# Token transform on even and odd tokens apart: 145 of 289 outputs computed, the rest by sum and difference

## The chip, the cores and the metric

The kernel runs on one core of one Trainium2 chip. The metric is the device time in microseconds (us); lower is better. A profile of one execution gives, beside it, the span from the first to the last instruction and what each engine did. The engines are PE (matrix multiply, with its weight loads shown as PEld), DVE (vector), ACT (scalar), POOL (GpSimd) and SP (which here only issues DMAs).

## What is computed

Two blocks follow each other. The first is attention within chunks of 64 tokens: q, k and v have shape (8 batches, 8 heads, 576 tokens, 64). The second takes the result as x with shape (8, 576, 512), mixes it by the real part of a two-dimensional Fourier transform, over tokens and over features, and puts a normalized two-layer MLP on top:

```python
scores = q_chunk @ k_chunk.T / sqrt(64)          # 64 x 64 for each chunk and head
x      = softmax(scores) @ v_chunk               # heads side by side: (8, 576, 512)
u      = x + real(fft(fft(x, axis=1), axis=2))
un     = (u - mean(u)) / sqrt(var(u) + 1e-6)     # over the 512 features
out    = u + relu(un @ w_ch1) @ w_ch2            # w_ch1 512 x 2048, w_ch2 2048 x 512
```

All of it is fp32 on the chip. The two weight matrices arrive as doubles and are rounded to fp32 on the chip.

## The kernel before, in words

**Tiles.** A tile is 128 tokens of one batch in 128 partitions, with 512 features. Of the 576 tokens of a batch, chunks 0 to 3 make two LO tiles, chunks 8 to 5 two HI tiles (tokens run the other way, and features mirrored), and chunk 4 is half of a RE (rest) tile that two batches share. That is 36 tiles: 16 LO, 16 HI, 4 RE. `CH` is 64, `NM` 2, `NQ` 289, `NL` 256, `HQ` 128, `DV` 65.

**Attention** of a tile (`attention_early` for batch 0, `attention` for the others) has four parts: `att_T` transposes q and k, `att_S` multiplies them (L384), `softmax` and `exponential` work on DVE and ACT, `att_P` transposes the probabilities on PE and copies them from PSUM with ACT (L416), and `att_V` multiplies by v (L432) and scales the result into `xall` with DVE. L384 and L432 use 64 x 64 pieces of the PE array: for each pair of heads four matmuls, two in rows by two in columns. From batch 2 on, `att_V` of a tile is followed directly by `att_S` of the next one.

**Fold.** `shift` puts token rows in order so that LO token t stands beside HI token 576 - t. `fold` then adds and subtracts LO and HI and their mirrored features, which makes `pm`: four blocks of 128 features (T = 0 to 3) for i = 0, 1, and `pm_rest` for the rest tile. One more column of `pm` holds the middle feature. It runs on POOL, on DVE for batch 1 and for the last fold of batch 0.

**Token transform.** `fourier(b)` multiplies each block by a table of cosines (T = 0, 1) or sines (T = 2, 3) for tokens 0 to 288 (L652). The rest tile contributes with 64 rows, the middle column with one-column matmuls whose results lie in four partition groups of one PSUM bank. ACT then copies the four results into `zf` (tokens 1 to 256) and `zr` (tokens 257 to 288 with their mirror) in L678 to L688, and `mixed` (L700) does the feature transform from those. The four results use both buffers of the PSUM pool `ps_t` and the double bank of `ps_a`. Batch 0 has its own version, `fourier_early`, whose copies are divided between ACT and DVE, with matmuls on zeros (`keep_warm`, L1167) put between the parts of the start.

**Tables.** `load_tables` brings the tables in by DMA on SP's queue, `turn_tables` (L252 to L254, ACT) turns their tokens round into `tk`.

**MLP and the order of the work.** Each group of four tiles goes through `mlp`: group 0 with plain products in both layers, group 1 in the first layer, all others with a seven-product scheme on half matrices (`up_halves`, L1040, and `down_halves`, L1089), whose operands are combined on DVE, ACT and POOL and whose weight pieces come from DRAM through `fetch`. The order is written out by hand: after each step of the MLP the loop at L1213 advances the work of a later batch (attention, three empty steps, `fourier`) by as many steps as are due between two times in `ready_at`. `fourier` gives control back after the products of T = 0 and 1, after the copies, and after each `mixed`. Weight rounding (`round_weight`, L308 to L323 on DVE, L300 to L306 on ACT) also runs from this loop until all pieces are done, at about 154 us.[...]

**Stores.** `store` writes a finished tile: one DMA for LO, two for HI, and for each half of a RE tile one of 63 rows and one of a single row (L882, L883). All are on SP's queue, but for half of the last group's RE stores, which are on ACT's. The last group, the four RE tiles, ends the kernel.

Of the kernel before, what the change touches and what calls it, by code (L numbers as in the profile page):

```python
# [16 lines left out]
def kernel(  # L17
# [67 lines left out]
    tk = const.tile([128, NM + 1, 2, NQ], FP32, name="tk")  # L85
# [84 lines left out]
    more_v = one_p.tile([128, 4 * NL + 64], FP32, tag="zf", name="more_v")  # L170
# [53 lines left out]
    def load_tables():  # L224

        t = start[:, 0:(NM + 1) * 2 * NQ].rearrange("p (i r f) -> p i r f", i=NM + 1, r=2)
        for c in range(2 * NM):  # L230
            (i, r0), (j, p0) = divmod(c * CH, 128), divmod((NC - 1 - c) * CH, 128)
            nc.sync.dma_start(out=t[r0:r0 + CH, i], in_=seq_tab[p0:p0 + CH, j])
        for r0 in (0, CH):
            nc.sync.dma_start(out=t[r0:r0 + 1, NM], in_=seq_tab[0:1, 0])
            nc.sync.dma_start(out=t[r0 + 1:r0 + CH, NM], in_=seq_tab[1:CH, NM])
        for i in range(2):
            nc.sync.dma_start(out=first_rest[32 + 32 * i:33 + 32 * i, 0:DM], in_=dim_tab[0:1, 1 + 2 * i, :])
# [9 lines left out]

    def turn_tables():
        t = start[:, 0:(NM + 1) * 2 * NQ]
        a, b = tk.rearrange("p i r f -> p (i r) f"), t.rearrange("p (i f) -> p i f", f=NQ)  # L250
        for c in range(2 * NM):
            nc.scalar.copy(a[:, :, c * CH:(c + 1) * CH], b[:, :, (c + 1) * CH:c * CH:-1])  # L252
        nc.scalar.copy(a[:, :, NL:NL + 1], b[:, :, 0:1])
        nc.scalar.copy(a[:, :, NL + 1:NQ], b[:, :, NL + 1:NQ])  # L254
# [157 lines left out]
    def att_P(n):  # L412
        ex = es.pop(n)
        pt = turn(lambda j: ex[:, j].rearrange("p e k -> p (e k)"))
        t = one_p.tile([128, NJ, 128], FP32, tag="pT", name="pT")
        nc.scalar.copy(t, pt)  # L416
        pT[n] = t

    def att_V(n):
# [5 lines left out]
        else:  # L425
            xp = ps_a.tile([128, 2, 512], FP32, tag="att", name="xp")
            xp = [xp[:, e] for e in range(2)], xp
        for j in range(NJ):
            for e in range(2):
                for c in range(2):  # L430
                    r0, t0 = e * CH, c * CH
                    nc.tensor.matmul(  # L432
                        out=xp[0][e][t0:t0 + CH, j * DV:(j + 1) * DV],
                        lhsT=a[r0:r0 + CH, j, t0:t0 + CH],
                        rhs=b[r0:r0 + CH, c, j, :],
                        start=True,
                        stop=True,
                    )
# [25 lines left out]
    def shift_early(i):  # L464
# [3 lines left out]
        if i == 0:  # L468
            nc.gpsimd.tensor_copy(kept, lows[1][0:1])
            nc.gpsimd.tensor_copy(lows[1][0:1], lows[1][CH:CH + 1])  # L470
            nc.gpsimd.tensor_copy(lows[1][CH:CH + 1], rest)
        else:
            nc.scalar.copy(rest, lows[0][0:1])
            nc.scalar.copy(lows[0][0:1], lows[0][CH:CH + 1])
            nc.scalar.copy(lows[0][CH:CH + 1], kept)

    def shift(b):
# [6 lines left out]
        for i in range(NM):  # L484
            eng.dma_start(out=t[2 * i:2 * i + 2, 0:DM], in_=lows[i][0:CH + 1:CH, 0:DM])
        eng.dma_start(out=t[2 * NM:2 * NM + 1, 0:DM], in_=rest)
        for i in range(NM):
            eng.dma_start(out=lows[i][0:CH + 1:CH, 0:DM], in_=t[2 * i + 1:2 * i + 3, 0:DM])
        eng.dma_start(out=rest, in_=t[0:1, 0:DM])

    def fold(b, i):
# [5 lines left out]
        else:  # L497
            two = one_p.tile([128, 2 * (HM + 1)], FP32, tag="two", name="two")
        if i < NM:
            pm = two_p.tile([128, DM + 1], FP32, tag="pm", name="pm")  # L500
# [5 lines left out]
        else:  # L506
            pm = two_p.tile([128, 2 * HQ + 1], FP32, tag="pm_rest", name="pm_rest")
# [10 lines left out]
        if i < NM:  # L518
# [3 lines left out]
            to = pm[:, 3 * HQ:DM + 1:HQ]  # L522
        else:
            for T, op in enumerate((ALU.add, ALU.subtract, ALU.subtract, ALU.add)):
                to = pm[T % 2 * CH:T % 2 * CH + CH, T // 2 * HQ:T // 2 * HQ + HQ]
                eng.tensor_tensor(out=to, in0=near[:, T // 2], in1=far[:, T // 2], op=op)
            to = pm[CH:, HQ:2 * HQ + 1:HQ]
        eng.tensor_copy(to, two[p, HM + 1 + HQ:HQ - 1:-HM - 1])
        pms[b, i] = pm

    def attention_early():
# [33 lines left out]
        turn_tables()  # L565
# [78 lines left out]
    def fourier(b):  # L644
        h = b % 2
        zf = one_p.tile([128, 4 * NL + 64], FP32, tag="zf", name="zf")
        zf = zf[:, 0:4 * NL].rearrange("p (t f) -> p t f", t=4)
        pm = [pms.pop((b, i)) for i in range(NM + 1)]

        def product(T, i, out_, lhsT, start, stop, cols=slice(0, NQ)):  # L650
            p = slice(0, 128) if i < NM else slice(T % 2 * CH, T % 2 * CH + CH)
            nc.tensor.matmul(  # L652
                out=out_, lhsT=lhsT[p], rhs=tk[p, i, T // 2 if T != 5 else 0, cols],
                start=start, stop=stop, skip_group_check=True,
            )


        z = [ps_t.tile([128, 512], FP32, tag="pt", name="z") for _ in range(2)]
        more = ps_a.tile([128, 2, 512], FP32, tag="att", name="more_z")
        z += [more[:, k] for k in range(2)]  # L660
        for T in range(4):
            for i in range(NM):
                product(T, i, z[T][:, 0:NQ], pm[i][:, T * HQ:(T + 1) * HQ], i == 0, False)
            if T == 1:
                yield
        for T in range(4):
            product(T, NM, z[T][:, 0:NQ], pm[NM][:, T // 2 * HQ:(T // 2 + 1) * HQ], False, True)

        mids = []
        for g, c0 in enumerate(range(0, NQ, NS)):  # L670
            c1 = min(c0 + NS, NQ)
            mids.append((c0, c1, z[2][32 * g:32 * g + 1, NQ:NQ + c1 - c0]))
        for i in range(NM + 1):
            for c0, c1, out_ in mids:
                one = pm[i][:, DM:DM + 1] if i < NM else pm[i][:, 2 * HQ:2 * HQ + 1]
                product(5, i, out_, one, i == 0, i == NM, slice(c0, c1))
        for T in range(4):
            nc.scalar.copy(zf[:, T, :], z[T][:, 0:NL])  # L678
            nc.scalar.copy(zr[:, T, h, 0:NQ - NL], z[T][:, NL:NQ])
            upper, mirrored = zr[:, T, h, NQ - NL:CH], z[T][:, NQ - 2:NL:-1]  # L680
            nc.scalar.activation(out=upper, in_=mirrored, func=ACTF.Copy, scale=1.0 if T < 2 else -1.0)
            for c0, c1, from_ in mids if T == 2 else ():
                n = max(0, min(c1, NL) - c0)
                if n > 0:
                    nc.scalar.copy(zf[0:1, T, c0:c0 + n], from_[:, 0:n])
                if c1 > NL:
                    nc.scalar.copy(zr[0:1, T, h, 0:NQ - NL], from_[:, n:])
                    nc.scalar.copy(zr[0:1, T, h, NQ - NL:CH], from_[:, NQ - 2 - c0:NL - c0:-1])  # L688
# [38 lines left out]
    def fourier_early():  # L727
# [3 lines left out]
        zf = one_p.tile([128, 4 * NL + 64], FP32, tag="zf", name="zf")  # L731
        zf = zf[:, 0:4 * NL].rearrange("p (t f) -> p t f", t=4)
        pm = [pms.pop((0, i)) for i in range(NM + 1)]
        z = [ps_t.tile([128, 512], FP32, tag="pt", name="z") for _ in range(2)]
        more = ps_a.tile([128, 2, 512], FP32, tag="att", name="more_z")
        z += [more[:, k] for k in range(2)]
        mid = ps_f.tile([128, 512], FP32, tag="ff", name="mid")
        mids = [(c0, min(c0 + NS, NQ)) for c0 in range(0, NQ, NS)]
        order = (1, 0, NM)
        for i in order:  # L740
            at_ = {"start": i == order[0], "stop": i == order[-1], "skip_group_check": True}
# [554 lines left out]
```

## Time and profile before

| what | value |
|---|---|
| device time, median of 3 runs | 1091.47 us (1090.56 to 1092.83) |
| span of the profiled execution (the page gives no other time of its own for it) | 1089.0 us |
| mean granted PE clock, share of full speed | 0.998 |
| PE busy | 1070.4 us, 98% |
| DVE busy | 577.2 us, 53% |
| ACT busy | 299.2 us, 27% |
| POOL busy | 280.3 us, 26% |
| DMA | 192.73 MB, mean 177 GB/s |
| chain that ended last: L1089 and L1040 together | 20% + 17% + 15% + 13% |
| same chain: L652, the token products | 2% + 1% |

Times in the profile's rows are in us from the start of the span. A row of the timeline has start, duration, engine, line, operation, out<-in by the program's names, shapes, and how many instructions were merged into it; a note in brackets is idle time of that engine just before, and what ended it. [...]the distance between starts is what one costs in a stream. "PEclk" is the granted clock.

### The profile page before, as it was taken

To read this page: it belongs to the slowest core of one execution; us is meant where nothing else is said; L and a number is where in the kernel's file an instruction comes from. 1 tells how busy PE (TensorE), PEld (TensorE's weight loads), DVE (VectorE), ACT (ScalarE), POOL (GpSimd) and SP (SyncE) were. 2 spreads that over 40 slices of the span, in tenths; PEclk is the share of its full clock that TensorE was granted. 3 is DMA by queue.
4 is the path that set the end of the run, shared out by engine and by line. 5 is a ranking of instruction groups with operands and counts; after the bars stand their busy time and mean duration, and the time that the engine had idled before them with its cause. 6 is when DMAs were issued, how large, how long until landed. Compare 5 with 4: busy or idle time off the path is not lost.

```text
span 1089.0 us, 18837 instructions
## 1 busy us (share of the span) xinstructions
PE 1070.4 (98%) x7018; PEld 848.7 (78%) x7018; DVE 577.2 (53%) x1258; ACT 299.2 (27%) x730; POOL 280.3 (26%) x403
## 2 busy tenths in 40 slices
PE   8999999999999999999999999999999999999998
PEld 6644454446888888888888888888888888888887
DVE  4899987314566355663556455735663534323411
ACT  4788453222113310322022212321133103101300
POOL 4301002444405140153114220514051401210140
PEclk9999999999999999999999999999999999999999
DMA  7777556679575637692668357854653455446232
GB/s 167 224 222 175 158 162 227 171 239 308 178 203 167 198 136 206 189 255 95 191 184 253 124 165 223 206 170 152 197 185 90 147 190 163 120 154 211 78 116 78
DMA packets 147970, 192.73 MB, mean 177 GB/s; under 512 B 66126, under 2 KB 104014, under 8 KB 140712
## 3 DMA queue, kind: packets, MB, share of 16 engines
q1 hardware_dynamic: 145620, 190.20, 58.4%
q8 instruction: 56, 0.92, 0.4%
q0 software_dynamic: 512, 0.68, 0.3%
q10 hardware_dynamic: 1748, 0.66, 0.2%
q14 instruction: 34, 0.28, 0.1%
HBM read 167.22 MB, written 24.12 MB: 176 GB/s over the span
## 4 chain that ended last, share of the span: by engine, by line
PE 89%; DVE 4%; ACT 2%; DMA 2%; SPq 2%; issue 1%; POOL 0%; DVEq 0%; ACTq 0%
PE pb L1089 20%; PE pa L1040 17%; PE pa L1089 15%; PE pb L1040 13%; PE up L973 4%; PE up L953 3%; PE pt L333 3%; PE dn L994 3%; PE mix L700 2%; PE sc L384 2%; PE more_z L652 2%; PE xp L432 2%; PE z L652 1%; PE idle L1167 1%; DMA xall<-in_moe_w_ch_dram 1%; SPq L195 1%
## 5 line engine op out<-in xcount | busy, mean ns | idle before, releaser
L1040 PE MATMUL pa<-unT,wa 128*128 128x256 f32 x672 | 159.5, 380 | 1.1 <-DVE wa L1048 1.1
L1040 PEld LDWEIGHTS pa<-unT,wa 128*128 128x128 f32 x672 | 126.5, 190 | 18.9 <-DVE wa L1048 1.5
L941 POOL TENSOR_TENSOR h<-h 128x256 f32<-128x256 f32 x64 | 55.7, 877 | 269.5 <-PE pb L1040 150.5
L1089 PE MATMUL pa<-wb,h 128*128 128x256 f32 x512 | 115.6, 380 | 0.0
L1089 PE MATMUL pb<-wb,h 128*128 128x256 f32 x512 | 114.9, 379 | 0.0
L1040 PE MATMUL pb<-wa 128*128 128x256 f32 x448 | 106.6, 381 | 0.0
L1089 PEld LDWEIGHTS pa<-wb,h 128*128 128x128 f32 x512 | 96.1, 190 | 13.5 <-issue 0.5
L1089 PEld LDWEIGHTS pb<-wb,h 128*128 128x128 f32 x512 | 96.3, 190 | 12.6
L1040 PEld LDWEIGHTS pb<-wa 128*128 128x128 f32 x448 | 84.2, 190 | 11.6 <-DVE h L1056 0.2
L994 PE MATMUL dn<-wb,h 128*128 128x512 f32 x128 | 58.4, 605 | 0.9 <-ACT h L964 0.9
L1046 DVE TENSOR_TENSOR wa<-pb,wa 128x256 f32<-128x256 f32 x56 | 23.5, 423 | 65.5 <-ACT wa L1045 65.5
L1089 PE MATMUL pb<-wb,yall 128*128 128x256 f32 x256 | 58.2, 381 | 0.0
L1089 PE MATMUL pa<-wb,yall 128*128 128x256 f32 x256 | 57.9, 380 | 0.0
L1089 PE MATMUL pb<-wb 128*128 128x256 f32 x256 | 57.7, 379 | 0.0
L973 PE MATMUL up<-unT,wa 128*128 128x512 f32 x128 | 56.8, 596 | 0.0
L1045 ACT COPY wa<-pa 128x256 f32<-128x256 f32 x56 | 20.8, 372 | 125.1 <-PE pa L1040 125.1
L1040 PE MATMUL pa<-wa 128*128 128x256 f32 x224 | 53.5, 382 | 0.0
L717 POOL TENSOR_TENSOR xall<-y,xall 128x513 f32<-128x513 f32 x14 | 21.3, 1518 | 125.3 <-DVE y L711 125.3
L1040 PE MATMUL pb<-unT,wa 128*128 128x256 f32 x224 | 52.9, 379 | 0.0
L1089 PEld LDWEIGHTS pa<-wb,yall 128*128 128x128 f32 x256 | 47.7, 190 | 6.4
L1089 PEld LDWEIGHTS pb<-wb,yall 128*128 128x128 f32 x256 | 47.7, 190 | 6.3
L1089 PEld LDWEIGHTS pb<-wb 128*128 128x128 f32 x256 | 47.6, 190 | 5.9
(250 smaller groups left out, 1685.0 us busy)
## 6 DMA issues: line engine op xcount, KB each, us to landing
wb<-s SPq DMA_DIRECT2D x56, 1024.0 KB
wa<-s SPq DMA_DIRECT2D x196, 256.0 KB
xall<-in_moe_w_ch_dram SPq DMA_DIRECT2D x22, 512.0 KB
q<-in_q_dram SPq DMA_DIRECT2D x96, 112.0 KB
k<-in_k_dram SPq DMA_DIRECT2D x96, 112.0 KB
v<-in_v_dram SPq DMA_DIRECT2D x124, 64.0 KB
yall<-in_moe_w_ch_dram SPq DMA_DIRECT2D x10, 512.0 KB
s<-wb SPq DMA_DIRECT2D x20, 256.0 KB
```

The lines of the kernel that those rows point to most:

```text
L333: nc.tensor.transpose(pt[:, j, :], src(j), ident)
L384: nc.tensor.matmul(out=sc[t0:t0 + CH, e, j * CH:(j + 1) * CH], lhsT=a[r0:r0 + D, 2 * j + c, 0:CH], rhs=b[r0:r0 + D, 2 * j + c, 0:CH], star ...
L432: nc.tensor.matmul(out=xp[0][e][t0:t0 + CH, j * DV:(j + 1) * DV], lhsT=a[r0:r0 + CH, j, t0:t0 + CH], rhs=b[r0:r0 + CH, c, j, :], start=Tru ...
L652: nc.tensor.matmul(out=out_, lhsT=lhsT[p], rhs=tk[p, i, T // 2 if T != 5 else 0, cols], start=start, stop=stop, skip_group_check=True,)
L700: nc.tensor.matmul(out=mix[:, cols], lhsT=zt[:, T], rhs=tab, start=(T == 0), stop=(T == 3), skip_group_check=True,)
L941: nc.gpsimd.tensor_tensor(out=h1[:, m, hi], in0=h1[:, m, lo], in1=h1[:, m, hi], op=ALU.subtract)
L953: nc.tensor.matmul(out=up, lhsT=w1[:, kk, m * 128:(m + 1) * 128], rhs=unT[:, kk], start=(kk == 0), stop=(kk == KD - 1), skip_group_check=True,
L973: nc.tensor.matmul(out=up, lhsT=w1[:, kk, m * 128:(m + 1) * 128], rhs=unT[:, kk], start=(kk == 0), stop=(kk == KD - 1),)
L994: nc.tensor.matmul(out=dn, lhsT=h1[:, m, s * 128:(s + 1) * 128], rhs=w2[:, m, :], start=(m == 0), stop=(m == KF - 1),)
L1040: nc.tensor.matmul(out=dst, lhsT=w[:, kk, r], rhs=rhs[o][:, kk], start=(o in (0, 1) and kk == 0), stop=(kk == 1), skip_group_check=True,)
L1046: nc.vector.tensor_tensor(out=b, in0=pbs[r][:, 0], in1=a, op=ALU.add)
L1089: nc.tensor.matmul(out=dst, lhsT=lhs[:, m], rhs=w[:, m], start=(o in (0, 2) and m == 0), stop=(m == HF - 1), skip_group_check=True,)
```

## The change

- **Tokens apart.** ACT's copy in `att_P` orders the probabilities so that even tokens of both chunks come first, odd ones last. `att_V` of LO and HI tiles then puts even tokens in partitions 0 to 63 of the tile and odd ones in 64 to 127, with 32-column weights (eight matmuls for each pair of heads instead of four). In a RE tile, even and odd tokens are apart within each half.
- **Products.** `z_sets` multiplies the even half and the odd half on their own, 64 rows each (32 rows in the rest tile), for outputs 0 to 144 only. Even results go to the double bank of `ps_a`, odd ones to the two buffers of `ps_t`.
- **Joining.** ACT copies the odd results to SBUF (`z_odd`). DVE adds them to the even ones for outputs 0 to 144 and subtracts for the others, which lie mirrored (`z_joined`: one operation of 580 columns, two of 290). ACT copies the middle rows (`z_middle`) and makes `zf` and `zr` (`z_tile`, `z_rest`), in which even tokens again come first.
- **Middle column.** `fold` makes one more column by a sign for each partition, so that the middle column gives sum and difference from the same products.
- **Steps.** `fourier` now does all products and `z_odd` in its first step, and the joining and copies in its second. The number of steps is the same.
- **Tables.** Every second row and 145 columns are loaded straight into `tk`; `turn_tables` is gone.
- **Stores.** Rows of a chunk are written in two DMAs, even and odd. For HI the odd ones are on ACT's queue; a RE half has one DMA of 32 rows and one of 31, and one DMA for both first rows.

The diff, cut to its core:

```diff
-    tk = const.tile([128, NM + 1, 2, NQ], FP32, name="tk")
+    NE = NQ // 2 + 1
+    tk = const.tile([128, NM + 1, 2, NE], FP32, name="tk")
+    sign = const.tile([128, 2], FP32, name="sign")
...
         for r0 in (0, CH):
-            nc.sync.dma_start(out=t[r0:r0 + 1, NM], in_=seq_tab[0:1, 0])
-            nc.sync.dma_start(out=t[r0 + 1:r0 + CH, NM], in_=seq_tab[1:CH, NM])
+            nc.sync.dma_start(out=tk[r0:r0 + 1, NM], in_=seq_tab[0:1, 0, :, 0:NE])
+            nc.sync.dma_start(out=tk[r0 + 1:r0 + CH // 2, NM], in_=seq_tab[2:CH:2, NM, :, 0:NE])
+            nc.sync.dma_start(out=tk[r0 + CH // 2:r0 + CH, NM], in_=seq_tab[1:CH:2, NM, :, 0:NE])
...
-        nc.scalar.copy(t, pt)
+        nc.scalar.copy(
+            t.rearrange("p j (c r i) -> p (j c) r i", c=2, r=2), pt.rearrange("p j (c i r) -> p (j c) r i", c=2, r=2)
+        )
...
+        parts = [(c, CH * c, CH * c, CH) for c in range(2)]
+        if kind(n) != RE:
+            HC = CH // 2
+            parts = [(c, CH * r + HC * c, CH * c + HC * r, HC) for r in range(2) for c in range(2)]
         for j in range(NJ):
-            for e in range(2):
-                for c in range(2):
-                    r0, t0 = e * CH, c * CH
+            for c, t0, a0, rows in parts:
+                for e in range(2):
+                    r0 = e * CH
                     nc.tensor.matmul(
-                        out=xp[0][e][t0:t0 + CH, j * DV:(j + 1) * DV],
-                        lhsT=a[r0:r0 + CH, j, t0:t0 + CH],
+                        out=xp[0][e][t0:t0 + rows, j * DV:(j + 1) * DV],
+                        lhsT=a[r0:r0 + CH, j, a0:a0 + rows],
...
+        eng.tensor_tensor(out=pm[rows, m0 + 1:m0 + 2], in0=pm[rows, m0:m0 + 1], in1=sign[rows, int(i == NM):1 + int(i == NM)], op=ALU.mult)
...
-        turn_tables()
...
+    def z_sets(z, pm, i, first):
+        if i < NM:
+            sets = [[(T, r, CH * r, CH, T * HQ) for r in range(2)] for T in range(4)]
+        else:
+            sets = [[(2 * (r // 2) + s, r % 2, 32 * r, 32, s * HQ) for r in range(4)] for s in range(2)]
+        for T, r, p0, rows, d0_ in sum(sets, []):
+            p, o = slice(p0, p0 + rows), T % 2 * NE
+            nc.tensor.matmul(
+                out=z[r][T // 2][:, o:o + NE], lhsT=pm[i][p, d0_:d0_ + HQ],
+                rhs=tk[p, NM - 1 - i if i < NM else NM, T // 2],
+                start=first and T % 2 == 0, stop=False, skip_group_check=True,
+            )
...
+    def z_odd():
+        for k in range(2):
+            nc.scalar.copy(zs[0][:, 2 * k:2 * k + 2, 1], zs[2][k][:, 0:2 * NE].rearrange("p (t f) -> p t f", t=2))
+
+    def z_joined():
+        even = zs[1][:, :, 0:2 * NE].rearrange("p k (t f) -> p k t f", t=2)
+        z4 = zs[0].rearrange("p (k t) r f -> p k t r f", t=2)
+        nc.vector.tensor_tensor(out=z4[:, :, :, 0], in0=even, in1=z4[:, :, :, 1], op=ALU.add)
+        for k in range(2):
+            e, o = even[:, k], z4[:, k, :, 1]
+            a, b = (e, o) if k == 0 else (o, e)
+            nc.vector.tensor_tensor(out=o, in0=a, in1=b, op=ALU.subtract)
+
+    def z_middle(outs):
+        for g, out_ in enumerate(outs):
+            c0, c1 = halves[g % 2]
+            nc.scalar.copy(zs[0][0:1, 2, g // 2, c0:c1], out_[:, 0:c1 - c0])
...
+        z = z_space()
         for i in range(NM + 1):
+            z_sets(z, pm, i, i == 0)
+        outs = [z[0][0][32 * g:32 * g + 1, 2 * NE:] for g in range(4)]
+        for i in range(NM + 1):
+            mid_products(outs, pm, i, i == 0, i == NM)
+        z_odd()
+        yield
+        z_joined()
+        z_middle(outs)
+        for i in range(NM):
+            z_tile(zf, i)
+        z_rest(h)
         yield
...
             if kind(n) == RE:
-                eng = nc.scalar if n in groups[-1][1::2] and h else nc.sync
-                eng.dma_start(out=out[b, t0 + 1:t0 + CH, :], in_=o[r0 + 1:r0 + CH])
-                eng.dma_start(out=out[b, 0:1, :], in_=o[r0:r0 + 1])
+                eng = nc.scalar if last and h else nc.sync
+                eng.dma_start(out=out[b, t0 + 1:t0 + CH:2, :], in_=o[r0 + CH // 2:r0 + CH])
+                eng.dma_start(out=out[b, t0 + 2:t0 + CH:2, :], in_=o[r0 + 1:r0 + CH // 2])
             else:
-                nc.sync.dma_start(out=out[b, t0:t0 + CH, :], in_=o[r0:r0 + CH])
+                for r in range(2):
+                    p0 = CH * r + CH // 2 * h
+                    eng = nc.scalar if r else nc.sync
+                    eng.dma_start(out=out[b, t0 + r:t0 + CH:2, :], in_=o[p0:p0 + CH // 2])
+        if kind(n) == RE:
+            eng.dma_start(out=out[b - 1:b + 1, 0, :], in_=o[0:CH + 1:CH])
```

`z_tile` and `z_rest` make five ACT copies each (two of 256 columns for the first tile, three for the second; five small ones for the rest tile). `fourier_early` calls the same functions without the empty step between products and joining.

## The prediction

> **What bounds the kernel now.** I read the page first: busy time, then the chain of waits.
>
> ```profile
> span 1089.0 us, 18837 instructions
> ...
> PE 1070.4 (98%) x7018; PEld 848.7 (78%) x7018; DVE 577.2 (53%) x1258; ACT 299.2 (27%) x730; POOL 280.3 (26%) x403
> ...
> PE 89%; DVE 4%; ACT 2%; DMA 2%; SPq 2%; issue 1%; POOL 0%; DVEq 0%; ACTq 0%
> ```
>
> PE bounds it, so work taken off PE counts wherever nothing else is late. Next the PE timeline of one batch's token transform (batch 2). An fp32 matmul is recorded as two passes (x8 is four instructions).
>
> ```profile
> 257.31 2.11 PE L652 MATMUL z<-tk,pm 128*128 128x289 f32 x8
> ...
> 262.71 2.11 PE L652 MATMUL more_z<-tk,pm 128*128 128x289 f32 x8
> 264.75 0.76 PE L652 MATMUL z<-tk,pm_rest 64*128 64x289 f32 x4
> 265.34 0.66 PE L652 MATMUL more_z<-tk,pm_rest 64*128 64x289 f32 x4
> 265.93 0.43 PE L652 MATMUL more_z<-tk,pm 128*1 128x73 f32 x16
> ...
> 266.52 3.72 PE L1089 MATMUL pa<-wb,yall 128*128 128x256 f32 x16
> ```
>
> No idle time stands beside these rows. The 64-row matmuls take half as long per pass as the 128-row ones: 8 passes start within 1.18 us (264.75 to 265.93), against 1.95 us of chain time for 8 full ones. The two row halves overlap.
>
> Three places are not PE's alone. The first is the start, before MLP work exists to hide anything:
>
> ```profile
> 36.54 0.81 DVE L323 TENSOR_TENSOR wa<-wa,power 128x512 f32<-128x512 f32 x1
> ...
> 38.01 3.89 PE L774 MATMUL early_xp<-start,zf 128*128 128x256 f32 x16
> ...
> 40.19 0.69 DVE L798 TENSOR_TENSOR xall<-early_xp,xall 128x512 f32<-128x512 f32 x1
> ```
>
> The second is batch 1, where PE waits for ACT's copies, and the clock falls after it (last row: window, PE busy, PEclk, DMA share, GB/s):
>
> ```profile
> 152.06 0.49 PE L700 MATMUL mix<-ce,zr 128*128 128x129 f32 x2 [1.12 <-ACT zr L681]
> ```
> ```profile
> 151.11 0.69 DVE L323 TENSOR_TENSOR wb<-wb,power 128x512 f32<-128x512 f32 x1
> ```
> ```profile
> 154.10:157.50 3.40, 3.40 (x8) 0.57 0.49 171
> ```
>
> The third is the end, where only the stores of the last group remain:
>
> ```profile
> 1084.32 0.42 DVE L1109 TENSOR_TENSOR wb<-pb,wb 128x256 f32<-128x256 f32 x1 [3.10 <-PE pb L1089]
> 1084.77 0.28 SPq L882 DMA_DIRECT2D out_dram<-wb  x1
> ```
>
> [...]0.09 us between the last full pass and 264.75, and some 0.10 us of exposed weight load. [...]the loads of two row halves start 7 ns apart in the trace and the next two 108 ns later, so they overlap. [...]Here 0.57 stands in the window after one in which PE was busy 1.46 of 3.4 us. [...]the two 63-row and two 1-row stores after 1084.5 end with 20 four-byte completion writes, 2 x 9 + 2 x 1.[...]
>
> **The change part by part.** The sum is made against the profiled span, 1089.0 us; the median, 1091.47, is 2.5 us more and I take that as the constant around it.
>
> *Token products, batches 2 to 7.* Before: 1.95 + 1.95 + 0.09 + 1.18 + 0.59 (the middle rows, 265.93 to 266.52) = 5.76 us. After: a 256-column pass takes 3.45/16 = 216 ns and a 128-column one 110 ns (mix), so 145 columns take 124 ns. Sixteen 64-row instructions in pairs make 16 such slots, 1.98 us. Eight 32-row ones in fours make 4, 0.50 us. Two mode entries of 0.19, a drain of 0.09 and the same middle rows, 0.59: 3.54 us. Saved 2.2 us a batch, 13.2 in six. Bounds: 2.3[...]. New DVE and ACT work lies under MLP steps: evacuation takes 5 us after the products, and two steps of 3.45 us (even batches; in odd ones 1.7 + 6.9) pass before mix.
>
> *Attention times V.* 32 of 36 tiles get twice the instructions, 64 x 32 tiles. Before, 32 passes took 0.52 us (xp at 471.49, sc at 472.00), and sc followed in the same mode without a drain. After, 64 passes in eight tiles at once need the same stream time (eight slots of 57 ns); passes start 7 ns apart in the trace and 8 x 7 fits. A mode change to sc is new: 0.09 + 0.05 = 0.14 us. The timeline has 25 such successions after 180 us; 3 are rest tiles, which keep their form, 2 lie in other waits: 20 x 0.14 = 2.8, plus 0.5 for imperfect packing, 3.3 us. Bounds: 0, and 24 x 0.46 = 11 us if only four tiles run at once.
>
> *Start.* The table copies on ACT (29.65 to 31.77) go; nothing is gained, since six idle matmuls hold PE to 31.70 and the fold on DVE ends at 33.42. The products end 1.9 us sooner (36.1), also for nothing: DVE is in L323 until 37.35. Then come, in series, three DVE joins (580, 290, 290 columns[...]; queued 0.09 closer): 1.5 us to 38.9. Four one-row ACT copies as L685 (0.85 for four) to 39.75; two ACT copies of 256 columns, 0.71, to 40.5; eight passes of 216 ns, to 42.3. L798 starts at 42.45 instead of 40.19: +2.3. PE has been idle 4.4 us by then; a halved clock adds 1.7; I take three chances in four, +1.3. The chain from L798 to 50 us has no slack and PE is full after it, so 3.6 stays. Bounds 2.0 and 4.5.
>
> *Batch 1.* The joins queue behind DVE's weight rounding (L323, free at 151.73): to 153.2; ACT's row copies to 154.1, its tiles and rest copies to 156.0. Mix then starts 3.9 us after 152.06, but before it had waits inside; its end moves from 155.26 to 157.3. PE, whose products are 2.2 us shorter, has idled 7 us, so the cold clock costs 1.9 instead of 0.9. Sum +3.0; bounds 1.3 and 4.5. Batch 1's own product gain is lost in this wait.
>
> *Stores.* Rest tiles' 63-row DMAs become 32 + 31 rows. [...]Each of four tiles puts 2 x 31 + 4 + 1 = 67 packets of 2 KB on it. In the packet records such packets follow each other every 80 ns on an engine: 268 x 0.080 = 21.4 us. The first store is issued at 1074.41, its packets come 0.8 us later, tiles follow every 3.45 us, so the engine never empties: it ends near 1096.7 where the last packet now ends at 1087.42: +9.3. Nothing covers it. Bounds 0.3 (spread as now, one more issue) and 10. The other stores: HI's odd halves move to ACT's queue (two issues of 0.3 to 0.6 us a tile), where they wait for DVE's L1109; queued behind are copies for the next MLP step, L1045, needed over 2 us later: nothing. LO's second DMA on SP: nothing, SP waits more than it issues. Sign products, 0.1 to 0.3 us each on POOL and DVE, lie under attention, except 0.1 at the start, included. Table loads: twelve DMAs instead of ten, half the bytes; [...]first read at 35: nothing. Eight more memsets ahead of the first matmul: 0.1, within the start's bounds. The strided reads of ACT's pT copy: between 0 and 1 us at the start, taken as 0.
>
> Sum: -13.2 + 3.3 + 3.6 + 3.0 + 9.3 = +6.0 us: **1097.5 us**.
>
> **Rivals.** A, not slower: the 31-row stores do not serialize. For it: the last stores now take 1.9 us in all; against it: the nine engines counted for 63 rows. The tail costs 0.3, the sum is -3.0, 1088.5 us. It is faster than before from a tail under 3.3 us. B: V's eight tiles run four at a time; the trace never shows more than four. Sum +16.5 less the 0.5: 1107.5. C: start and batch 1 are cheaper (warm clock, copies overlapping): 2.0 + 1.3 instead of 6.6, 1094.2. D: the halves' weight loads serialize at 124 ns slots: gain 4.5, not 13.2: 1106.2. The trace's loads 7 ns apart speak against it.
>
> **How the numbers follow.** Forecast 0.50 (1095 to 1101), A 0.12, B 0.08, C 0.20, D 0.07, else 0.03. Two in ten may lie outside: most of A below, B and half of D above, so 1091.5 to 1105. About 0.2% (2.2 us) is what a measurement can tell from no change. Faster: most of A, 0.10; same: the rest of A and the low edge of C, 0.08; slower 0.82.
>
> **What would show it.** Right: 16 + 8 products of 145 columns in about 2.9 us; L798 near 42.5 to 44; mix of batch 1 near 156 (plus the start's shift); after the last L1109 over 10 us of SP waiting at low DMA share. Wrong: the span ending 5 us after the last matmul as now (A); V stretches of 1 us (B).

## The result, and the profile after

The changed kernel took 1116.03 us (median of 4 runs, 1115.46 to 1118.34), the kernel before 1091.15 beside it: a ratio of 1.0232, 95% interval 1.0217 to 1.0246. The forecast was 1097.5. The profiled spans are 1114.1 and 1089.0 us: 25.1 us more. The page of the changed kernel, first lines and chain of waits:

```profile
span 1114.1 us, 21417 instructions
...
PE 1066.1 (96%) x8234; PEld 848.5 (76%) x8234; DVE 588.3 (53%) x1290; ACT 305.4 (27%) x712; POOL 284.2 (26%) x423
...
PE 83%; DMA 5%; DVE 5%; SPq 3%; ACT 2%; issue 1%; POOL 0%; DVEq 0%; ACTq 0%
```

PE does 4.3 us less than before, yet the span is 25 us longer. In the chain PE fell from 89% to 83%, and DMA rose from 2% to 5%. So the loss is in waits. The timeline of batch 2's products, changed kernel:

```profile
273.90 0.39 PE L659 MATMUL more_z<-tk,pm 64*128 64x145 f32 x1
273.91 0.39 PE L659 MATMUL z<-tk,pm 64*128 64x145 f32 x1
274.13 0.28 PE L659 MATMUL more_z<-tk,pm 64*128 64x145 f32 x1
274.14 0.28 PE L659 MATMUL z<-tk,pm 64*128 64x145 f32 x1
274.25 0.28 PE L659 MATMUL more_z<-tk,pm 64*128 64x145 f32 x1
...
276.08 0.39 PE L659 MATMUL more_z<-tk,pm_rest 32*128 32x145 f32 x1
...
277.38 0.91 PE L1137 MATMUL pa<-wb,h 128*128 128x256 f32 x3
```

The two halves start 0.01 us apart. After the first pair, which takes 0.22, the pairs follow each other every 0.12 us. That makes 3.48 us for a batch, where 5.76 were needed and 3.54 predicted. Now the start, batch 1 and the end:

```profile
40.40 0.75 DVE L689 TENSOR_TENSOR zs<-more_z,zs 128x580 f32<-128x580 f32 x1
42.39 0.75 ACT L710 COPY zf<-zs 128x256 f32<-128x256 f32 x2
43.19 6.56 PE L815 MATMUL early_xp<-start,zf 128*128 128x256 f32 x16 [4.57 <-ACT zf L710]
...
157.37 0.43 DVE L306 TENSOR_SCALAR wb<-xall 128x512 uint32<-128x512 uint32 x1 [0.84 <-DMA xall<-in_moe_w_ch_dram]
...
159.98 0.75 DVE L689 TENSOR_TENSOR zs<-more_z,zs 128x580 f32<-128x580 f32 x1
164.67 0.80 PE L764 MATMUL mix<-ce,zr 128*128 128x129 f32 x2 [8.28 <-ACT zr L725]
...
1098.12 0.42 DVE L1157 TENSOR_TENSOR wb<-pb,wb 128x256 f32<-128x256 f32 x1 [3.10 <-PE pb L1137]
...
1104.44 0.54 ACTq L933 DMA_DIRECT2D out_dram<-wb  x1
```
```profile
1106.00:1110.00 4.00, 0.00 (x0) 0.00 (x0) 0.00 (x0) 0.00 (x0) 0.00 (x0) 0.50 0.07 26
1110.00:1114.10 4.10, 0.00 (x0) 0.00 (x0) 0.00 (x0) 0.00 (x0) 0.00 (x0) 0.50 0.03 13
```

L815 takes 6.56 us (PEclk 0.51 between 45 and 49 us) where L774 took 3.89; batch 1's joins stand on DVE behind a weight piece that waited for its own DMA; and from 1106 us on the DMA share is 0.07 and less, which is one DMA engine in 16.

To see where each us arose I compare the starts of the same MLP pass in both traces (3768 passes each). The shift is 6.9 us at the first pass, 7.6 at pass 180, 11.5 at pass 240 (after batch 1's first mix), 13.8 at the last, 25.1 at the end. Between pass 240 and the last I sorted PE's time by operation, counting gaps of over 0.45 us between starts (0.9 in the mix) as waits. How such a gap is split between pass and wait moves the row of waits by about 1 us:

| passes 240 to 3768 | predicted | measured |
|---|---|---|
| token products | -13.2 | -13.7 |
| attention times V, and the scores after it | +3.3 | +8.1 |
| other passes | 0 | +0.4 |
| waits | 0 | +7.5 |

By the same count the kernel before waits 7.0 us in this stretch, so these 7.5 come on top. The waits view of PE from 172 to 1085 us, changed kernel, and what stands behind the first of them in the timeline:

```profile
PE sc L382 <- DVE rd L449: 3.5, 1, 3.5
PE pa L1088 <- DVE wa L1096: 2.5, 1, 2.5
PE pb L1088 <- DVE wa L1096: 0.9, 1, 0.9
```
```profile
201.67 2.49 ACTq L931 DMA_DIRECT2D out_dram<-o  x4
203.39 0.33 SPq L968 DMA_DIRECT2D s<-xall  x1
225.35 1.08 DVE L350 STREAM_TRANSPOSE kT<-k 128x512 f32<-128x512 f32 x1 [11.04 <-DMA k<-in_k_dram]
226.48 1.14 PE L382 MATMUL sc<-kT,qT 64*64 64x64 f32 x32 [3.48 <-DVE rd L449]
```

PE waits for DVE, DVE stands in a transpose that waits for k, and k came late from SP's queue. The stall costs more than its 3.48 us, since the granted clock is 0.50 from 226.4 to 229.8 us: over this place the MLP passes fall back from 11.9 to 17.3 us behind the kernel before. SP itself stood waiting for stores. Its waits for landed stores from 172 to 1085 us sum to 44.2 us in 27 waits, against 21.7 in 8 before. The largest of the changed kernel:

```profile
SPq L978 <- DMA out_dram<-wb: 10.8, 6, 2.5
SPq L918 <- DMA out_dram<-wb: 7.9, 2, 4.4
...
SPq L968 <- DMA out_dram<-o: 4.1, 1, 4.1
```

Why should a load wait for a store of other data? In the built program every DMA of SP's and ACT's queues takes one of eight semaphores, in turn, and waits until the DMA eight places ahead of it has landed. The trace has it: of the 908 DMAs of the two queues each semaphore has 113 or 114. For 821 of the 900 that have a successor on their semaphore, all 16 semaphore updates come before that successor goes out; for the other 79 the trace has fewer than 16 updates. s<-xall at 203.39 has the semaphore of ACT's store of 201.67, and was let go when that landed, at 203.32. POOL's 16 DMAs take turns on eight others, two on each. Sorted by the store that held the semaphore, the 44.2 us are 22.6 for HI halves on ACT's queue and 21.5 for LO stores; the 21.7 us of the kernel before are all for LO stores. What is new is thus the waits for HI's stores.

### The profile page after: what moved, and what is told of

Same layout as the page of the kernel before. It is cut to its first block, busy times and chain, and to the rows that moved or that the text cites. A ratio compares the mean times of both kernels' runs of the same rounds, so it can differ in the third digit from the quotient of the medians.

```text
span 1114.1 us, 21417 instructions
## 1 busy us (share of the span) xinstructions
PE 1066.1 (96%) x8234; PEld 848.5 (76%) x8234; DVE 588.3 (53%) x1290; ACT 305.4 (27%) x712; POOL 284.2 (26%) x423
## 4 chain that ended last, share of the span: by engine, by line
PE 83%; DMA 5%; DVE 5%; SPq 3%; ACT 2%; issue 1%; POOL 0%; DVEq 0%; ACTq 0%
PE pb L1137 20%; PE pa L1088 16%; PE pa L1137 15%; PE pb L1088 12%; PE up L1021 4%; PE up L1001 3%; PE dn L1042 3%; PE pt L331 2%; PE mix L764 2%; PE xp L436 2%; PE sc L382 1%; PE more_z L659 1%; SPq L210 1%; DMA xall<-in_moe_w_ch_dram 1%; DMA k<-in_k_dram 1%; DMA q<-in_q_dram 1%
## 5 line engine op out<-in xcount | busy, mean ns | idle before, releaser
L1137 PEld LDWEIGHTS pa<-wb,h 128*128 128x128 f32 x512 | 96.0, 190 | 13.7 <-issue 0.9
L1021 PE MATMUL up<-unT,wa 128*128 128x512 f32 x128 | 57.9, 605 | 0.0
L1001 PE MATMUL up<-unT,wa 128*128 128x512 f32 x108 | 49.8, 600 | 0.7 <-ACT h L1012 0.6
```

Of the source, the lines that this page charges most:

```text
L1001: nc.tensor.matmul(out=up, lhsT=w1[:, kk, m * 128:(m + 1) * 128], rhs=unT[:, kk], start=(kk == 0), stop=(kk == KD - 1), skip_group_check=True,
L1021: nc.tensor.matmul(out=up, lhsT=w1[:, kk, m * 128:(m + 1) * 128], rhs=unT[:, kk], start=(kk == 0), stop=(kk == KD - 1),)
L1137: nc.tensor.matmul(out=dst, lhsT=lhs[:, m], rhs=w[:, m], start=(o in (0, 2) and m == 0), stop=(m == HF - 1), skip_group_check=True,)
```

## The experiments

Each ratio stands against the kernel before on the same chip; the changed kernel's own 1116.0 is the reference for what an edit gave. The kernel before took 1089.8 to 1091.8 us (medians) beside these runs, so a gain of under 2 us is not told from none in this way. f1, f2, f3, g1 and g2 leave rows of the output in wrong places; they only put a price on a part.

### One part at a time

**e1_stores**, the tail.
```diff
-                eng.dma_start(out=out[b, t0 + 2:t0 + CH:2, :], in_=o[r0 + 1:r0 + CH // 2])
+                eng.dma_start(out=out[b, t0 + 2:t0 + 34:2, :], in_=o[r0 + 1:r0 + 17])
+                eng.dma_start(out=out[b, t0 + 34:t0 + CH:2, :], in_=o[r0 + 17:r0 + CH // 2])
```


> The changed kernel with each 31-row store of a rest tile cut in a 16-row and a 15-row store. Theory, the 31 rows of a store all go through one DMA engine (25 packets of 2 KB in every 2 us after the last matmul, 80 ns each): the tail shrinks to what it was, so 10 to 11.5 us less than the changed kernel's 1116.0, about 1105. Rival, the tail comes of the order in which the two queues issue: more stores to issue, no gain or up to 1 us more, 1116 to 1117.

Measured 1106.99 (1.0139, 1.0122 to 1.0156), 9.0 less, a little under the 10 to 11.5 expected; the span is 10.6 shorter. The windows after its last MLP pass end with the span, at 1103.5:

```profile
1098.00:1101.00 3.00, 0.00 (x0) 0.00 (x0) 0.00 (x1) 0.00 (x0) 0.00 (x0) 1.00 0.26 73
1101.00:1103.50 2.50, 0.00 (x0) 0.00 (x0) 0.00 (x0) 0.00 (x0) 0.00 (x0) 0.61 0.07 19
```

So the 31-row store was the tail: in the changed kernel's packet records 24 to 26 packets of 2 KB start in every 2 us from 1105 to 1111, on both queues together, one every 80 ns, as on a single engine. In the kernel before, the last 63-row store has 9 such packets in every 80 ns (1086.83 to 1087.07).

**e2_queue**: both HI halves on SP's queue.
```diff
-                    eng = nc.scalar if r else nc.sync
+                    eng = nc.sync
```


> The changed kernel with both halves of the HI stores on SP's queue, as before the change. Theory, a store on ACT's queue couples the queues: SP's next DMA takes the semaphore of ACT's store, which waits for DVE's addition, so SP stands still 4.1 us at 199 to 203 and the load of k lands 4 us late; with the stores on SP that wait and PE's 3.65 us stall at 226 go to what they were (1.5 us at 211 in the kernel before): 4 us less, about 1112. Rival, k is late because SP has twice as many stores ahead of it: then it is later still, 1116 to 1118.

1114.52 (1.0200, 1.0182 to 1.0219), 1.5 less (3.5 by the ratios), between the two cases. At that place the theory holds: the wait at 203 went, k was transposed at 221.85 instead of 225.35, and PE's stall fell from 3.48 to 1.32. But SP now spends longer in the stores, and the four loads of k take 6.35 us to issue. 4.8 of it are waits for two LO stores, whose semaphores the last two loads take over:

```profile
204.54 2.87 SPq L931 DMA_DIRECT2D out_dram<-o  x4
...
212.94 6.35 SPq L197 DMA_DIRECT2D k<-in_k_dram  x4
```

A stall of 2.63 us came at 241 instead, and PE's waits after pass 240 stay 8.3 us above the kernel before. SP's waits for stores still sum to 35.1 us, now all for LO stores (21.5 in the changed kernel). So it isn't ACT's queue alone; the theory fell as an account of the sum.

**e3_join**: batch 1's joins one step earlier.
```diff
         z_odd()
-        yield
+        if b > 1:
+            yield
         z_joined()
 ...
         z_rest(h)
+        if b == 1:
+            yield
         yield
```


> The changed kernel with batch 1's joins and copies issued right after its products, one step earlier, ahead of the weight piece that waited for its DMA until 157.37. Theory, that piece is what holds the joins: they start at 152.9 instead of 159.98, mix starts within 2 us of 156.4, where the MLP pass before it ends, and PE's stall of 8.45 us shrinks to under 2: 6 to 8 us less, 1108 to 1110. Rival, the chain of joins and copies itself is the stall (164.9 less 160.0 is 4.9 us of it): 2 to 3 us less, 1113 to 1114.

1116.57 (1.0226, 1.0211 to 1.0242): nothing. Yet the mechanism is right. From PE's waits:

```profile
PE sc L382 <- DVE rd L449: 6.1, 1, 6.1
...
PE mix L767 <- ACT zr L725: 1.9, 1, 1.9
```

The mix's wait fell from 8.3 to 1.9, and at pass 240 the kernel was 5.8 us ahead of the changed one. Then the wait for k grew from 3.5 to 6.1, others followed, and at pass 1000 the lead was 0.2. Something paces this stretch that PE can't outrun.

**e4_v32**: the kernel before with V in 32-column parts.
```diff
+        parts = [(c, CH * c, CH) for c in range(2)]
+        if kind(n) != RE:
+            HC = CH // 2
+            parts = [(c, CH * c + HC * r, HC) for r in range(2) for c in range(2)]
         for j in range(NJ):
-            for e in range(2):
-                for c in range(2):
...
+            for c, t0, rows in parts:
+                for e in range(2):
...
```


> The kernel before, with attention times V in parts of 32 columns for all tiles but the rest tiles, as in the changed kernel, and nothing else. The prediction's step says +3.3 us (0.14 a tile for the change of mode and 0.5). What the trace of the changed kernel shows: 0.79 us a tile instead of 0.52, and 0.04 more in the scores after it, in 24 tiles, 0.16 in the 5 of batch 1 before 130 us, and two waits of 0.6 us among the early tiles: 7.4 + 0.8 + 1.5, so +9 to +10, 1100 to 1101. Four tiles at a time instead of eight would be +14 or more.

1095.29 (1.0036, 1.0025 to 1.0048), +3.5: near the +3.3 of the prediction, by luck, since the terms are others, and not the +9 to +10 that I expected of this run. PE's passes cost 7.5 us more after pass 240, and 3.2 us of waits that the kernel before has there are gone. A tile takes 0.79 us instead of 0.52. In the pass records of the changed kernel the first 32 passes start within 0.245 us (the predicted rate), the other 32 within 0.377; the change of mode to the scores costs the predicted 0.14.

**e5_warm**: idle matmuls at the start.
```diff
             mid_products(outs, pm, i, i == 1, i == NM)
+        keep_warm(7)
         z_odd()
```


> The changed kernel with seven idle matmuls (3.7 us) after the early products, while PE waits for the joins. Theory, the clock fell to half from 42.1 to 48.9 us because PE had nothing to do: it stays at full speed, the first mix's 16 matmuls take 1.9 us instead of 3.8, the first up pass comes at 50.5 to 51 instead of 52.8, and nothing between there and 130 us has slack, so all later marks up to batch 1 move by 2 us. At the end: 1114 if it is kept, 1115.5 if the waits for loads take it.

1115.92 (1.0240, 1.0220 to 1.0260): nothing in the end. At the start it did what it should; the same 16 matmuls, in its timeline:

```profile
43.05 3.89 PE L816 MATMUL early_xp<-start,zf 128*128 128x256 f32 x16 [0.96 <-ACT zf L710]
```

3.89 us instead of 6.56; the first MLP pass came 1.9 us earlier. The lead lasts to pass 200 and is gone by pass 330, in waits.

### Which part makes the waits

**f1_stores**: all stores as in the kernel before; the edits of g1_lo and g2_hi below, and for rest tiles:
```diff
-                eng.dma_start(out=out[b, t0 + 1:t0 + CH:2, :], in_=o[r0 + CH // 2:r0 + CH])
-                eng.dma_start(out=out[b, t0 + 2:t0 + CH:2, :], in_=o[r0 + 1:r0 + CH // 2])
+                eng.dma_start(out=out[b, t0 + 1:t0 + CH, :], in_=o[r0 + 1:r0 + CH])
+                eng.dma_start(out=out[b, 0:1, :], in_=o[r0:r0 + 1])
...
-        if kind(n) == RE:
-            eng.dma_start(out=out[b - 1:b + 1, 0, :], in_=o[0:CH + 1:CH])
```

> The changed kernel with every store as in the kernel before: one DMA of 128 rows for a LO tile, two of 64 rows on SP for a HI tile, 63 rows and 1 row for a half rest tile. The rows of a chunk are then stored in the order in which the tile holds them, even tokens ahead of odd ones; all else is computed. Between MLP pass 240 and the last one PE waited 7.5 us more in the changed kernel than before. Theory S, the stores made those waits (more issues on SP, semaphores shared with ACT's queue): they go with the tail, 11 + 5 to 7 us less, 1098 to 1100. Theory T, the waits are what SP's queue of loads allows once PE works faster in between, whatever the stores: only the tail goes, 1104 to 1106.

1095.3 (1.0043, 1.0021 to 1.0065): 20.7 less. PE's waits are 0.9 us more than before instead of 7.5. That is Theory S; the gain is even 3 us beyond its range.

**f2_v64**: V in 64-column parts again.
```diff
-        if kind(n) != RE:
-            HC = CH // 2
-            parts = [(c, CH * r + HC * c, CH * c + HC * r, HC) for r in range(2) for c in range(2)]
```


> The changed kernel with attention times V in 64-column parts for all tiles; the rows of a tile then lie by chunks, even ahead of odd inside each, so that the tokens of the transform and of the stores are not the right ones; all else is computed. The passes of V and of the scores after it took 8.1 us more between pass 240 and the last, 0.7 more in passes 1 to 240, and some 1.5 in the early tiles. If all of it is on the path: 10 us less, 1106. If half of it lies beside waits for loads that are there anyway, as in the kernel before with V alone changed (7.5 us of passes, 3.2 us less of waits): 1109 to 1112.

1115.5 (1.0230, 1.0208 to 1.0253): 0.5 less, which neither case had. V's passes gave back their time, and waits grew from 7.5 to 13.6 us more than before.

**f3_products**: the edits of f1_stores and f2_v64 at once.

> Both of the last two at once: of the change only the token products, the joins and the tables are left, with rows in the wrong order in the stores and in the tiles. The products save 13.7 us after pass 240. Theory S: the start and batch 1 cost 5.5 and 4, the waits are those of the kernel before, so 1091 + 9.5 - 13.7, 1086 to 1088, faster than before. Theory T, waits for loads take part of what the products save: 1090 to 1093.

1089.1 (0.9987, 0.9977 to 0.9997), between the two theories. Waits after pass 240 are 0.4 us above the kernel before, as S says; PE's last pass comes 1.1 us before that kernel's. The products, with the joins and tables, thus win back the 11.5 us that this kernel has lost by pass 240, and 1.1 more.

**g1_lo** and **g2_hi**: one kind of store each.
```diff
-            to = out[b, c * CH + 1:c * CH + 129, :].rearrange("(c p) d -> c p d", c=2)[:, ::-1]
-            for r in range(2):
-                nc.sync.dma_start(out=to[:, r::2], in_=o[r * CH:(r + 1) * CH])
+            to = out[b, c * CH + 1:c * CH + 129, :].rearrange("(c p) d -> c p d", c=2)
+            nc.sync.dma_start(out=to[:, ::-1], in_=o)
```


> The changed kernel with a LO tile's 128 rows stored by one DMA, as in the kernel before (rows of a chunk in the tile's order); HI and rest stores as in the changed kernel. With all stores reverted PE's waits after pass 240 fell from 10.8 + us to 4. If LO's second DMA makes them (both LO stores run on two DMA engines, 6 to 7 us each pair, and SP's later loads take over their semaphores): 5 to 9 us less than 1116, 1107 to 1111. If HI's four DMAs make them: 1115 to 1117.

```diff
-                for r in range(2):
-                    p0 = CH * r + CH // 2 * h
-                    eng = nc.scalar if r else nc.sync
-                    eng.dma_start(out=out[b, t0 + r:t0 + CH:2, :], in_=o[p0:p0 + CH // 2])
+                nc.sync.dma_start(out=out[b, t0:t0 + CH, :], in_=o[r0:r0 + CH])
```


> The changed kernel with a HI tile's rows stored by two DMAs of 64 rows on SP, as in the kernel before (rows of a chunk in the tile's order); LO and rest stores as in the changed kernel. If HI's four DMAs on two queues make PE's waits after pass 240: 5 to 9 us less than 1116, 1107 to 1111. If LO's second DMA makes them: 1115 to 1117. With the four HI stores all on SP the waits stayed (8.3 us more than before), so if it is HI, it is their number and not their queue.

g1_lo 1111.69 (1.0199, 1.0184 to 1.0215), 4.3 less, between its two cases, with waits still 6.2 us more. g2_hi 1106.44 (1.0160, 1.0135 to 1.0184), 9.6 less, waits 0.1 more. It is HI's four DMAs of 32 rows, mostly. (The two engines of LO's stores, in the changed kernel's packet records: while such stores land, from 218.1 to 221.1 us, 12 or 13 packets of 2 KB start in every half us, two every 80 ns.)

**g3_pool**: the same four DMAs, two of them from POOL's queue.
```diff
-                    eng = nc.scalar if r else nc.sync
+                    eng = nc.gpsimd if r else nc.sync
```


> The changed kernel with HI's odd halves stored from POOL's queue instead of ACT's. In the built program all DMAs of SP's and ACT's queues take turns on eight semaphores, each waiting for the DMA eight places ahead of it to have landed; POOL's DMAs take turns on eight of their own. Theory L, HI's two further DMAs a tile use up those turns, so that loads of q, k and slabs wait for stores to land (SP stood 44.2 us in waits for stores, 21.7 in the kernel before): they go as with HI stored by two DMAs, 7 to 10 us less than 1116, 1106 to 1109. Rival, the four transfers of 32 rows themselves delay the others in the DMA engines, or POOL's queue is held by DVE's additions: no gain, 1114 to 1118.

1106.39 (1.0158, 1.0132 to 1.0185), 9.6 less (8.1 by the ratios). The profiled run was the fastest of its four, 1103.7; they reach to 1110.6. The transfers are the same and as many, and SP issues no fewer; only the semaphores and the queue of two of them differ. PE's waits from 172 to 1085 us, whole:

```profile
PE sc L382 <- DVE kT L350: 0.7, 2, 0.5
PE xp L436 <- ACT unT L899: 0.4, 1, 0.4
```

SP's waits for stores fell from 44.2 to 24.0 us, and none of these is for a HI store. That the number of transfers alone is the cause is thus excluded, and so are SP's issues. What could still share in it is ACT's queue, held by DVE's additions in the changed kernel; but e2 took that away too and won little. This leaves the turns on the shared semaphores as the main cause; no run changed the semaphores alone, without the queue.

### The start, and a better version

**h1_pad64** and **h1_pad512**: padding ahead of one tile (8 and 88 elements).
```diff
+    pad = const.tile([128, 88], FP32, name="pad")
     start = one_p.tile([128, KF * 512], FP32, tag="big", name="start")
```


> The changed kernel with 32 bytes of padding ahead of the tile start, into which the first q, k and tables are loaded. In the changed kernel that tile begins 32 bytes past a multiple of 64 (address 139424), in the kernel before at a multiple of 512 (142848); between 12 and 16 us the same 256-byte packets took 29 ns instead of 19, and PE waited for k at 11.9 and 16.4 us. Theory A, writes that don't begin at a multiple of 64 bytes are slower: with the pad (139456) the packets take 19 ns, the scores of the third early tile begin near 16.4 instead of 17.7, and the first MLP pass comes 1.0 to 1.5 us earlier, 51.3 to 51.8. Theory B, the place does not matter: no change in these marks, 52.3 to 52.9. The whole: 1114 to 1117 under both, since the waits for loads take such gains.

> As the last, with 352 bytes of padding, so that the tile begins at a multiple of 512 (139776). If 64 bytes are what matters, as the last; if only whole 512 bytes count, this one alone shows packets of 19 ns and the first MLP pass at 51.3 to 51.8. Theory B: 52.3 to 52.9, packets near 29 ns. The whole: 1114 to 1117.

1116.95 (1.0248, 1.0224 to 1.0272) and 1113.02 (1.0210, 1.0185 to 1.0235). The pad moves this tile and all behind it. With the first, at a multiple of 64 bytes, nothing is won: packets of 29.1 ns, first MLP pass at 53.5. With the second, at a multiple of 512, they took 20.1 ns and the pass came at 50.4, 2.4 us earlier than in the changed kernel, about twice what was expected. In its timeline the third early scores are where the kernel before has them (16.37):

```profile
12.38 0.70 PE L383 MATMUL sc<-kT,qT 64*64 64x64 f32 x32 [1.02 <-ACT kT L371]
...
16.26 0.69 PE L383 MATMUL sc<-kT,qT 64*64 64x64 f32 x32
```

The early V's two breaks, of 0.71 and 0.67 us in the changed kernel (at 20.56 and 24.75), are gone too.

**g4_best**, **h2_best**, **i1_hi**, **i2_lo**: the edits of g3, e1, e3 and e5 together (g4); with them the larger padding and, at the start (h2),
```diff
-        round_weight(1, parts="t")
...
             z_tile(zf, i)
+        round_weight(1, parts="t")
         round_weight(1, put_off, "h")
```
and on top of h2 more stores on POOL's queue: all four of a HI tile (i1), or the second of a LO tile (i2).

> All repairs in one, outputs complete: HI's odd halves from POOL's queue, the 31-row stores cut in 16 and 15 rows, batch 1's joins one step earlier, seven idle matmuls at the start. Alone the first is expected to give 7 to 10 us, the second gave 9, the third 5.4 and the fourth 1.9 up to the first attention stretch, both lost again in waits for loads after it. If those waits are gone with the first, all add up: 1088 to 1092, no slower than the kernel before. If they only move: 1094 to 1098.

> The repaired kernel (HI's odd halves from POOL's queue, 31-row stores cut, batch 1's joins one step earlier, idle matmuls at the start), with the 352 bytes of padding and, at the start, the last three DVE steps of weight piece 0 behind the joins instead of ahead of them (they took from 37.7 to 40.4 us in the changed kernel, and DVE is idle after the joins). The repaired kernel was at 1093.5, with its first MLP pass at 50.5. Moving the three steps lets the joins begin at the products' end: 1.5 us earlier; the padding 1.3 us if theory A holds: first pass at 47.7 with both, 49.0 with one. If the gain stays: 1090.5 to 1092, the kernel before within its error; if waits for loads take it: 1093 to 1094.

> The last kernel (all repairs, 1090.8) with all four stores of a HI tile from POOL's queue: the shared eight semaphores then carry two stores a pair of tiles, the kernel before has three. In the last kernel PE still waited 4 us more after pass 240 than in the kernel before. Theory L (turns on the semaphores): the waits fall to at most what the kernel before has, PE ends 3 to 5 us earlier, 1086.5 to 1088.5, faster than before. Rival, POOL's queue, held by DVE's additions twice as long, delays its own work (folds, subtractions for MLP operands): 1091 to 1094.

> The same repaired kernel (1090.8) with the second store of a LO tile from POOL's queue as well (HI's odd halves stay there): SP carries one LO and two HI stores a pair, as many as in the kernel before. Theory L: waits as before or less, 1087 to 1089. Rival, LO's stores run on two DMA engines 6 to 7 us a pair, from either queue, and it is their slowness that loads wait for: 1090 to 1092.

g4_best 1093.54 (1.0029, 1.0019 to 1.0040); h2_best 1090.82 (1.0005, 0.9993 to 1.0017), first pass at 48.8; i1_hi 1087.44 (0.9971, 0.9961 to 0.9982); i2_lo 1086.75 (0.9963, 0.9952 to 0.9975). PE's waits after pass 240 against the kernel before: +1.6, +4.1, -1.4, -2.5 us. g4 falls between its two cases. In the profiled run of h2, one of its slowest, the 2.5 us that it wins on g4 by pass 240 go into waits again. In i1 and i2, where still fewer stores take turns with the loads, what start and batch 1 win is kept, and both beat both kernels.

**j1_before**, the control.
```diff
-                nc.sync.dma_start(out=out[b, t0:t0 + CH, :], in_=o[r0:r0 + CH])
+                nc.gpsimd.dma_start(out=out[b, t0:t0 + CH, :], in_=o[r0:r0 + CH])
```


> The kernel before, with its two HI stores a tile from POOL's queue and nothing else: the control for the two fastest kernels, which have the change, its repairs and stores from POOL. The kernel before waited 7.0 us on PE after pass 240 (3.3 in MLP passes, 1.2 and 2.5 around attention). If part of those waits is again turns on the shared semaphores, it gains too, 2 to 4 us, 1086 to 1088, and the lead of the repaired kernels comes of the queue alone. If they are others: 1089.5 to 1091, and the lead of 3 us is the changed transform's.

1088.14 (0.9978, 0.9966 to 0.9989). Its interval overlaps those of i1 and i2: that the changed transform beats the old one, each with stores on POOL's queue, is not shown. Nor does its profile, of one of its slower runs, show its gain: span 1088.8 against 1089.0, PE's waits 0.6 us less.

## Why the prediction was wrong

The direction and most mechanisms were right; the sum was 19 us short, and the result lies outside the range.

- **The step that failed** is the sentence on the other stores: HI's odd halves on ACT's queue, "needed over 2 us later: nothing", and LO's second DMA, "nothing, SP waits more than it issues". I looked at who is queued behind on ACT and at SP's free time, and not at what a DMA itself waits for before it is issued. In the changed kernel SP stands 22.6 us in waits for HI's stores on ACT's queue. g3 prices HI's part at 9.6 us of time (8.1 by the ratios), f1 all stores at 20.7, 9 to 11 of it the tail. The table's +7.5 us of waits is not even the whole: e3, e5 and f2 show that any time won elsewhere was taken by it as well.
- **Attention times V**: the mode change (0.14) was right, the packing was not: 0.13 a tile beyond it instead of 0.5 in all, 0.04 more in the scores; +8.1 us of passes instead of 3.3. Alone it still costs 3.5, since the kernel before waits there anyway; I had not counted that cover.
- **Start**, +6.9 instead of +3.6. V 1.3 (e4, first pass), which I had under V without placing it on the start's path; a tile moved off its 512 bytes 2.4, which was no step at all; cold clock 1.9 (e5; 0.50 from 42.1 to 48.9 us in the changed kernel) where I took 1.3 for 1.7, an estimate from the one such window of the trace before (0.57 from 154.1 us). If these add, 1.3 are left for joins and copies, where 2.3 stood. The 1.5 us for the joins were my estimate; they took 1.61 (40.40 to 42.01).
- **Batch 1**, +3.9 from pass 180 to 240 instead of 3.0. The step put the joins at 151.73 plus the start's shift; they began at 159.98, since the weight piece ahead of them came 8.3 us later (149.10 to 157.37), while PE, with shorter products, was ready 5.4 later. That this piece held them e3 shows. From 161.6 to 168.4 us the granted clock is 0.50, which by my estimate costs half of the 3.7 us from 164.67, the 1.9 us of the forecast.
- **Tail**, +11.3 instead of 9.3 by the trace, 9.0 by e1's median: right. That one engine takes all 31 rows was an assumption, which no run had shown by then.
- **Products**, 3.48 us a batch instead of 3.54: right. Rivals A, B and D are refuted by e1's tail, by 0.79 us a tile where B had 1, and by slots of 0.12 us; C by what start and batch 1 cost. D's 4.5 was my estimate: in the trace before, one pair of weight loads starts 108 ns after the other, and slots of twice that, 216 ns, would leave 0.74 us a batch, 4.5 in six. (A slip on which nothing hangs: B's sum takes its 0.5 off twice, and with 11 us in place of the 0.5 it comes to 1108.0.)

## What to carry to other kernels

Before calling a further DMA free, ask which semaphore it takes and which later load takes the same one, and not only how long its queue is idle (here HI's odd halves on ACT's queue cost 9.6 us, by g3). In this program that means: find the DMA eight places ahead of each load and ask when it lands. Look at the row count of every store (here the packets of 31 rows came one every 80 ns, as through one engine, and those of 63 rows nine), and, after a buffer changes size, at where the buffers behind it now begin (here 29 ns a packet instead of 19). A stretch that takes whatever you win beside it has a second bound; find that before adding gains up.

## What the hardware showed unexpectedly

- Loads of 256-byte rows into a tile that begins at a multiple of 512 bytes (142848 before, 139776 with the pad) took 19 to 20 ns a packet from 12 to 16 us; at 139424 and 139456, which are multiples of 32 and 64 only, 29. It is the written side that moved. The runs don't tell 128 or 256 from 512.
- Of the 64 passes of V on a tile the first 32 start within 0.245 us (7.9 ns apart), the other 32 within 0.377 (12.2 ns), in 21 of 24 tiles; the 32 passes of the kernel before take 0.480 (15.5 ns). What slows the second half was not tried.
